# Attention scores in four 64x64 tiles of the TensorE array, router logits in four column quarters, and a guard that keeps the second tile's last weights behind the keys

## Chip, cores, metric

One core of a Trainium2 chip. The metric is device time in microseconds (us) of that core. The kernel before takes 726.5 us (median of 4 runs, 723.9 to 727.3); two runs of one kernel usually agree within 1%.

In the profile, PE is the TensorE matmul engine, PEld its weight loads, DVE, ACT and POOL the vector, scalar and GpSimd engines, SP the engine that issues most DMAs. "L375" is line 375 of that kernel's file, so one line of code has other numbers in other kernels.

## The reference, cut to what matters

```python
# attention: B=8, H=8 heads, S=576, 64 numbers a head; window 32, in half the heads with dilation 4
scores = q @ k.T / sqrt(64); scores = where(mask, scores, -1e9)
attn = exp(scores - max) / sum
x = (attn @ v) laid out as (B, S, 512)
# mixture of experts, top 1 with a locality gate: 8 experts, 512 -> 1024 -> 512
logits = x @ w_gate; local = sigmoid(x @ w_local)
e = argmax(logits) if local < 0.5 else the expert of the position before
out = softmax(logits)[e] * (relu(x @ w1[e]) @ w2[e])
```

## The kernel before

It works through 32 head pairs n, two heads on 128 partitions, in 9 blocks of 64 queries with 96 keys each. Scores go into PSUM, DVE clamps them with the mask, ACT takes the exponential, PE multiplies with the values. Every second step transposes two pairs' output for the router. Logits come per group of two batches. When the first tokens are routed, 36 dense expert tiles follow. Attention takes some 140 us, the experts some 578.

```python
def load(n):                       # issued by SP four pairs ahead
    nc.sync.dma_start(out=kq, in_=qk[n])                 # 592 KB
    nc.sync.dma_start(out=vt[WIN:]..., in_=v[n])         # 292.5 KB
    loaded[n] = kq[:, :WIN + S], kq[:, WIN + S:], vt
...
def scores(n):
    for a, z in UNITS:                                   # blocks 0..4 and 5..8
        for i in range(a, z):
            for u in range(2):                           # the two heads: rows 0..63, 64..127
                h = slice(u * DH, (u + 1) * DH)
                matmul(sc[:KW, u, block i], lhsT=kt[h, 96 keys], rhs=qt[h, 64 queries],
                       tile_position=(u * DH, 0))
        DVE: pr = min(max(sc, -CEIL), mask);  ACT: pr = exp(pr)
...
def logits(g):                     # 1152 tokens in three column tiles of 384, in two banks
    for kk in range(DK):
        for lp, b, c, s, z in parts:                     # 384 or 192 tokens
            matmul(lp[c * LW:(c + 1) * LW, ...], lhsT=wg[:, kk], rhs=xt..., tile_position=(0, c * LW))
    # four ACT copies PSUM -> le, three transposes of le by PE ("lt")
...
for n in range(NPB + 2):           # the order of PE's work
    scores(n); turn((n - 3) // 2) if n is odd; values(n - 1)
    load(n + 4)
    fetch(6 if begun[0] else 1)    # expert weights
```

## Time and profile before

| | before |
|---|---|
| median | 726.5 us |
| profiled run: span, granted clock | 726.2 us, 0.997 |
| first hidden matmul of the experts ("experts begin") | 148.6 us |
| PE busy from 9.0 us to there | 133.3 of 139.6 us |
| PE's instruction fetch | 52 packets of 16 KB |

"Experts begin": the change touches only what comes before it, and in the chain in order of time it shows as the first row of 64 matmuls for hp. The stretch starts at 9.0 us because the first pair and most of the warm-up matmuls (L335) run before.

The busy times by stretch for that whole part of the kernel before (stretch, its length; busy us and records of PE, weight load, DVE, ACT, POOL; granted clock, DMA share, GB/s), then PE's waits up to there (engine, what it was to do, what it waited for; us in all, how often, the longest), then the row of PE's instruction queue on the page:

```profile
9.00:148.60 139.60, 133.25 (x2533) 114.51 (x2533) 98.42 (x299) 72.80 (x144) 33.47 (x32) 1.00 0.86 311
```
```profile
PE sc L373 <- DVE pr L380: 1.8, 4, 0.8
PE lt L496 <- ACT le L487: 1.7, 2, 0.8
...
PE sc L373 <- issue: 0.5, 1, 0.5
```
```profile
q8 instruction: 52, 0.85, 0.5%
```

PE is idle for 6.3 us of 139.6, at full clock from 11.2 us on, where the trace's clock record begins (the first pair's scores, before that, took 3.08 us and not 1.68). One wait of 0.5 us is marked "issue": PE stood still though no semaphore held it.

### The profile page before, as it was taken

Reading aid. Unit: us, or ns where it says so; the run is one execution under the profiler, and the core shown is the slowest. Engines: PE = TensorE matmul, PEld = TensorE weight load, DVE = VectorE, ACT = ScalarE, POOL = GpSimd, SP = SyncE. Lnnn points to the kernel's source line nnn. Section 1 sums busy time; section 2 is a strip of 40 time slices with the busy share of each in tenths; the row PEclk is TensorE's granted clock in tenths of the full one; section 3 lists DMA queues with packets and bytes.
Section 4 is the critical chain, followed back from the end, with each engine's and each line's share of the span. In section 5 each row is a group of like instructions: output and inputs, shape, how many; then the busy total and the mean of one; then the engine's idle time right before and its main releaser. Section 6 shows DMA issues by size and latency. Waiting matters only on the chain.

```text
span 726.2 us, 16502 instructions
## 1 busy us (share of the span) xinstructions
PE 709.1 (98%) x6354; PEld 536.4 (74%) x6354; DVE 191.4 (26%) x554; ACT 124.2 (17%) x233; POOL 211.3 (29%) x219
## 2 busy tenths in 40 slices
PE   8999999999999999999999999999999999999995
PEld 6978787967677777667766776677667767776773
DVE  3657597742239212110010101010110101010100
ACT  2646554512000000000100000001000000000000
POOL 2222210342332324313233323332333233323100
PEclk9999999999999999999999999999999999999998
DMA  9969787951683772535594171630169116211780
GB/s 335 338 235 328 230 285 300 402 217 59 185 312 107 229 267 44 162 130 178 176 318 158 53 256 33 203 110 29 33 210 325 38 33 213 100 30 36 216 297 15
DMA packets 37590, 131.22 MB, mean 181 GB/s; under 512 B 6686, under 2 KB 6814, under 8 KB 37504
## 3 DMA queue, kind: packets, MB, share of 16 engines
q1 hardware_dynamic: 29600, 110.68, 43.2%
q0 software_dynamic: 7904, 19.41, 9.6%
q8 instruction: 52, 0.85, 0.5%
q14 instruction: 34, 0.28, 0.1%
HBM read 207.37 MB, written 19.69 MB: 313 GB/s over the span
## 4 chain that ended last, share of the span: by engine, by line
PE 90%; DVE 5%; ACT 1%; issue 1%; DMA 1%; POOL 0%; POOLq 0%; DVEq 0%; ACTq 0%
PE hp L903 34%; PE yp L931 33%; PE sc L373 6%; PE pv L426 4%; PE tp L873 2%; PE hp L897 2%; PE lp L481 2%; PE yp L927 2%; PE put L767 2%; PE tp L452 2%; DVE pr L380 1%; DMA xg<-xd,dilated 1%; PE idle L335 1%; DVE x L432 0%; DVE by_place L749 0%
## 5 line engine op out<-in xcount | busy, mean ns | idle before, releaser
L903 PEld LDWEIGHTS hp<-xe,w1s 128*128 128x128 f32 x2304 | 262.9, 192 | 16.6 <-issue 16.3
L903 PE MATMUL hp<-xe,w1s 128*128 128x128 f32 x2304 | 264.8, 275 | 0.9 <-DVE xe L875 0.9
L931 PE MATMUL yp<-w2s,h 128*128 128x512 f32 x576 | 254.3, 593 | 0.0
L931 PEld LDWEIGHTS yp<-w2s,h 128*128 128x128 f32 x576 | 106.2, 190 | 118.2 <-issue 118.1
L856 POOL DMA_INDIRECT xg<-xd,plain x76 | 73.2, 964 | 296.8 <-PE yp L931 248.3
L907 ACT ACTIVATE h<-hp 128x512 f32<-128x512 f32 x76 | 45.4, 597 | 509.3 <-PE hp L903 481.1
L856 POOL DMA_INDIRECT xg<-xd,dilated x76 | 73.0, 961 | 57.4 <-PE yp L931 51.7
L939 DVE TENSOR_SCALAR y<-yp,gate 128x512 f32<-128x512 f32 x38 | 28.5, 751 | 216.4 <-PE yp L931 102.9
L875 DVE COPY xe<-tp 128x512 f32<-128x512 f32 x38 | 26.2, 690 | 214.6 <-PE tp L873 214.6
L940 POOL DMA_INDIRECT out_dram<-y,tok x38 | 38.7, 1019 | 79.3 <-DVE y L939 75.8
L373 PE MATMUL sc<-kq 64*96 64x64 f32 x1152 | 59.2, 252 | 2.5 <-DVE pr L380 1.8
L373 PEld LDWEIGHTS sc<-kq 64*96 64x96 f32 x1152 | 53.5, 165 | 8.0 <-DVE pr L380 2.7
L380 DVE SCALAR_TENSOR_TENSOR pr<-sc,mk 96x640 f32<-96x640 f32 x64 | 47.8, 747 | 40.7 <-PE pv L426 21.4
L383 ACT ACTIVATE pr<-pr 96x640 f32<-96x640 f32 x64 | 43.8, 685 | 61.3 <-DVE pr L380 56.7
L329 POOL COPY vt<-vt 32x1040 f32<-32x1040 f32 x25 | 26.1, 1045 | 75.1 <-DMA vt<-in_v_dram 62.5
L426 PE MATMUL pv<-vt,pr 96*64 96x65 f32 x1152 | 43.6, 225 | 0.5 <-ACT xt L457 0.2
L426 PEld LDWEIGHTS pv<-vt,pr 96*64 96x64 f32 x1152 | 37.5, 137 | 7.1 <-issue 3.8
L432 DVE TENSOR_TENSOR x<-pv,rec 128x320 f32<-128x320 f32 x64 | 26.9, 453 | 0.2
L873 PE MATMUL tp<-cst,xg 128*128 128x128 f32 x152 | 23.3, 275 | 0.8 <-DMA xg<-xd,dilated 0.8
L452 PE MATMUL tp<-cst,x 128*128 128x128 f32 x144 | 19.2, 278 | 0.0
L873 PEld LDWEIGHTS tp<-cst,xg 128*128 128x128 f32 x152 | 17.6, 141 | 1.9 <-DMA xg<-xd,dilated 1.1
L463 ACT COPY xt<-tp 128x288 f32<-128x288 f32 (+2 forms) x48 | 18.4, 564 | 0.9 <-PE tp L452 0.8
(178 smaller groups left out, 240.5 us busy)
## 6 DMA issues: line engine op xcount, KB each, us to landing
w1s<-in_w_dram SPq DMA_DIRECT2D x160, 512.0 KB
w2s<-in_w_dram SPq DMA_DIRECT2D x160, 512.0 KB
kq<-in_qk_dram SPq DMA_DIRECT2D x32, 592.0 KB
vt<-in_v_dram SPq DMA_DIRECT2D x32, 292.5 KB
xd<-x SPq DMA_DIRECT2D x16, 576.0 KB
xg<-xd,plain POOLq DMA_INDIRECT x76, 2.9
xg<-xd,dilated POOLq DMA_INDIRECT x76, 2.7
out_dram<-y,tok POOLq DMA_INDIRECT x38, 4.2
```

What stands on the lines that cost most here:

```text
L373: here[:] = [nc.tensor.matmul(sc[:KW, u, (i - a) * QB:(i - a + 1) * QB], lhsT=kt[h, i * QB:i * QB + KW], rhs=qt[h, i * QB:(i + 1) * QB], s ...
L380: nc.vector.scalar_tensor_tensor(pr[:, :, :w], sc[:KW, :, :w], -CEIL, mk[:, at:at + w].unsqueeze(1).to_broadcast([KW, 2, w]), Alu.max, Alu ...
L383: nc.scalar.activation(pr[:, :, :w], pr[:, :, :w], Act.Exp, scale=SCALE)
L426: here[:] = [nc.tensor.matmul(pv[u * QB:(u + 1) * QB, i - a], lhsT=pr[:, u, (i - a) * QB:(i - a + 1) * QB], rhs=vt[:, u, i], start=True, s ...
L452: nc.tensor.transpose(tp[:, :, i], x[:, c * w + i].rearrange("p g d -> p (g d)"), ident)
L856: i = nc.gpsimd.indirect_dma_start(out=xg[t][:, kk], out_offset=None, in_=xd if full == ROWS else xd[:full], in_offset=bass.IndirectOffset ...
L873: nc.tensor.transpose(tp[:, kk], x[:, kk], ident)
L903: here[:] = [nc.tensor.matmul(hp[:, m], lhsT=w1s[ps[0] % 2][:, at, kk], rhs=x[:, kk], start=(kk == 0), stop=(kk == DK - 1))]
L907: nc.scalar.activation(ht[t][:, half * FK // 2:(half + 1) * FK // 2], hp, Act.Relu)
L931: here[:] = [nc.tensor.matmul(yp, lhsT=h[:, m], rhs=w2s[ps[0] % 2][:, m], start=(m == 0), stop=(m == FK - 1))]
L939: nc.vector.tensor_scalar(y, yp, of_tile("gate", t), None, Alu.mult)
L940: nc.gpsimd.indirect_dma_start(out=out, out_offset=bass.IndirectOffsetOnAxis(ap=of_tile("tok", t), axis=0), in_=y, in_offset=None, bounds_ ...
```

## The change

Its intent: the score matmuls use two 64x96 pieces of the array at a time. Cut into 64 keys each, they would fill four 64x64 tiles at once, with shorter weight loads. The logits use three column tiles; four equal ones would take fewer rounds. The guard is to keep the second expert tile's last weights from going ahead of the keys.

```diff
-        loaded[n] = kq[:, :WIN + S], kq[:, WIN + S:], vt
+        loaded[n] = kq, kq[:, WIN + S:], vt
 ... scores
-                    here[:] = [nc.tensor.matmul(sc[:KW, u, (i - a) * QB:(i - a + 1) * QB],
-                                                lhsT=kt[h, i * QB:i * QB + KW], rhs=qt[h, i * QB:(i + 1) * QB],
-                                                start=True, stop=True, tile_position=(u * DH, 0))]
+                    for k in (0, QB):
+                        here[:] = [nc.tensor.matmul(sc[k:k + QB, u, (i - a) * QB:(i - a + 1) * QB],
+                                                    lhsT=kt[h, i * QB + k:(i + 1) * QB + k],
+                                                    rhs=qt[h, i * QB:(i + 1) * QB], start=True, stop=True,
+                                                    tile_position=(u * DH, k), skip_group_check=True)]
 ... logits
-        lps = [bank([P, NQ], "lp") for _ in range(2)]      (three column tiles, 384 + 192 tokens)
+        m = GS // 4
+        lp = bank([P, m], "lp")
         for kk in range(DK):
+            for c in range(4):
+                b, s = divmod(c * m, S)
+                nc.tensor.matmul(lp[c * LW:(c + 1) * LW], lhsT=wg[:, kk],
+                                 rhs=st["xt"][b][:, kk // CH, s:s + m, kk % CH], start=(kk == 0),
                                  stop=(kk == DK - 1), skip_group_check=True, tile_position=(0, c * LW))
+        (six ACT copies to le in place of four)
 ... main loop
-        fetch(1 if not begun[0] else 6)
+        if begun[0] or needs[0][:2] <= (1, False):
+            fetch(6 if begun[0] else 1)
```

(The logits' removed loop is left out.)

## The prediction

> **What bounds the kernel now.** I read the page, then the chain that ended last in order of time, then the busy times by stretch, then the trace's single records around the few waits that nothing explains. First the page:
>
> ```profile
> PE 709.1 (98%) x6354; PEld 536.4 (74%) x6354; DVE 191.4 (26%) x554; ACT 124.2 (17%) x233; POOL 211.3 (29%) x219
> ...
> L373 PE MATMUL sc<-kq 64*96 64x64 f32 x1152 | 59.2, 252 | 2.5 <-DVE pr L380 1.8
> L373 PEld LDWEIGHTS sc<-kq 64*96 64x96 f32 x1152 | 53.5, 165 | 8.0 <-DVE pr L380 2.7
> ...
> L426 PE MATMUL pv<-vt,pr 96*64 96x65 f32 x1152 | 43.6, 225 | 0.5 <-ACT xt L457 0.2
> ```
>
> PE is the bound: about 141 us of attention (slices 1 to 8), then 36 expert tiles that the change leaves alone. The program has 576 score matmuls; 1152 records say that an f32 matmul runs as two passes, each with its own weight load. The chain in order of time gives the length of each piece, 36 records a head pair n:
>
> ```profile
> 23.35 0.76 PE pv L426 x20
> 24.20 0.69 DVE pr L380
> 24.89 0.16 DVE rec L431 x2
> 25.05 0.57 DVE x L432 x2
> 25.62 0.14 issue
> 25.77 0.82 DVE pr L380
> 26.61 0.74 ACT pr L383
> 27.35 0.76 ACT xt L463 x2
> 28.15 0.69 PE pv L426 x16
> 28.84 1.68 PE sc L373 x36
> ...
> 36.22 1.17 PE sc L373 x24
> 37.38 0.50 issue
> 37.88 0.72 PE sc L373 x12
> 38.60 1.20 PE pv L426 x36
> ```
>
> Scores take 1.68 us a pair, values 1.20, transposes 1.13 in every second step. Two steps are 2 x 1.68 + 2 x 1.20 + 1.13 = 6.89 us of PE, and the chain's real pace is some 7.15. To see: in the step with a transpose (24.20 to 28.15) the chain leaves PE for DVE and ACT, and at 37.38 PE stands still with no semaphore awaited, in the middle of 36 like matmuls. That second wait is what I rest the prediction on.
>
> ```profile
> 29.00:42.00 13.00, 12.47 (x266) 11.44 (x265) 8.98 (x23) 6.37 (x12) 4.18 (x4) 1.00 1.00 381
> 42.00:58.00 16.00, 14.98 (x263) 11.48 (x263) 8.67 (x32) 9.14 (x20) 2.09 (x2) 1.00 0.63 214
> 98.00:114.00 16.00, 14.02 (x296) 12.59 (x296) 15.84 (x60) 8.31 (x17) 1.04 (x1) 1.00 0.89 315
> ```
>
> (Stretches: busy us of PE, weight load, DVE, ACT, POOL; clock; DMA share; GB/s.) DMA is nearly full while keys and values stream in, and DVE is full from 98 to 114.
>
> **What the Trainium skill says.** "TensorE: Matmul & The Clock Gate", section LDWEIGHTS: a weight load takes its columns divided by 1.2 GHz. The trace agrees: score records start in couples 6 ns apart (the two row tiles), and couples follow each 85 ns, with 96 columns (96/1.2 = 80, plus 5); the half tiles of L897 with 64 columns follow each 58 ns. "TensorEngine Tiling (Array Packing)", section Tiling Modes: 64x64 gives four tiles that load and compute on their own. Before shows only two or three at once: in the logits, parts in three column tiles start at 115.737, 115.743 and 115.750. "Runtime: NRT & Kernel Launch", section Instruction fetch mechanics: instructions come in 16 KiB blocks of 256, two blocks held, the next fetched while one runs, and this is mostly hidden. The trace agrees on the blocks and not on the hiding (below). "DMA: Bandwidth & Descriptors", section Queues, rings and completion order: an engine takes turns between its queues by packet. The trace shows fetch packets far later than one turn.
>
> **The instruction fetch.** The wait at 37.88 begins exactly 256 PE records after a like one at 31.10. PE's instruction queue moved one 16 KB packet from 28.67 to 29.81 and one from 35.53 to 36.54: PE went on 1.29 and 1.34 us after each. A third such wait stands in L897's dense half tiles, where DMA is quiet (packet end 706.91, on at 708.25, again 1.34):
>
> ```profile
> 37.88 0.56 PE L373 MATMUL sc<-kq 64*96 64x64 f32 x8 [0.50 <-issue]
> ```
> ```profile
> 708.25 0.92 PE L897 MATMUL hp<-xe,w1s 128*64 128x64 f32 x24 [0.45 <-issue]
> ```
>
> Laying the packets beside each 256th record of the trace, every block has its own packet, which starts after the block before has begun, and no block starts earlier than 1.29 us after its packet's end. From a block's begin to the next packet's start passes 1.05 us in the quiet case (708.25 to 709.30), 4.43 and 4.89 in the two attention stalls, 2.9 in the mean of the 20 attention blocks. It waits behind data: the packet at 42.77 came as the keys issued at 37.49 were landing (42.9). So a block can't take less than lag + 1.0 (packet) + 1.3: 3.35 us quiet, some 5.2 at the mean lag, 7 at worst. Now an attention block lasts 6.9 us, so this is hidden but for two waits.
>
> **The change part by part.** *Scores.* 1152 records of 96 weight columns become 2304 of 64, in four tiles. If four passes start together, a round takes 58 ns in place of 85; 18 rounds a pair: 18 x 27 = 0.48 us off, 1.68 becomes 1.20. Over 31 pairs 14.9 us of PE work; the first, at half clock (3.08 us), gives some 0.9 more. Not all of it can reach the end: in transpose steps the DVE-ACT chain above (3.95 us, nothing in it shortened) already sets the pace, so I allow 0.2 of 0.48 there. 15 x 0.48 + 16 x 0.2 = 10 us. *Logits.* Four tiles of 288 columns in place of 384 + 192 per tile: 8 rounds of some 250 ns for 8 of 340, 0.7 us a group; but the last rounds wait for ACT's copies of xt, and six copies out in place of four add 0.35 us of ACT (four took 1.5). Four groups at some 0.4: 1.6 us. *Weights behind the keys.* The compiled order of DMA issues on SP is the same, line for line, before and after: the new condition is never false where it would matter. Worth 0. Without anything else the sum is 10 + 0.9 + 1.6 = 12.5: 714 us.
>
> *What it adds.* 2304 more PE records (1152 matmuls, 1152 loads). Two steps hold 310 PE instructions now (144 scores, 144 values, 18 transposes, some 4 semaphore waits) and 454 after: 1.77 blocks for 1.21. From 13.9 to the experts' begin at 148.6 now run 19.6 blocks in 134.7 us; after, 28.3. Own work left: (134.7 - 10) / 28.3 = 4.4 us a block. Fetch: if PE slows, DMA has more air; I estimate the lag at 2.5, so 4.9 us a block. The longer of the two, both scattering by about 1 us, is some 5.1 in the mean: 28.3 x 5.1 = 145 us, 10 more than now. Less 1.6 and some of the 0.9: 726.2 + 10 - 2 = 734, and I say 735. The PE time gained is real but instructions arrive too slowly for it.
>
> **Rivals.** (a) *Fetch stays hidden*: lag falls to the quiet 1.05 us as the pace changes, a block needs only 3.35, and the gain is DVE-limited: 713 to 717. For it: the quiet lags are short, and waits for logits let DMA drain. Against: the streaming bytes are the same, and already now two blocks stalled. (b) *Four tiles run only in couples*: a round takes 2 x 58 = 116 ns, scores 2.2 us a pair, 31 x 0.56 = 17 us more: 743. Against it: three column tiles started within 13 ns in the logits. (c) *Fetch is worse than I think*: lag stays at 3.5, a block 5.8: 28.3 x 5.8 = 164, 29 more: 753. (d) *DMA bound*: two steps move 2 x (592 + 292.5) + 576 KB = 2.4 MB, 6.3 us at the 381 GB/s of the full stretch. That is below today's 7.15, and keys land 6 to 13 us before use from n = 4 on, so it takes a part of the gain at most: 716 to 718.
>
> **Range and chances.** The middle is 735; (a) and (d) draw the range to 716, (c) and (b) to 750. Faster by over 2% means under 711.7, beyond even (a) in full: 0.07. Slower by over 2% means over 740.7, a lag of 2.8 rather than 2.5: 0.29. Within: 0.64.
>
> **What would show it.** Right: in the score groups 2304 records, rounds of four starts some 6 ns apart and 58 ns a round; PE waits marked "issue" in attention rising from 2 to over ten, each 256 PE records apart and ending 1.3 us after a fetch packet; some 9 more fetch packets before the experts; the experts' first hidden matmuls later than 148.6; tile times there unchanged at 7.14 and 6.87 us. Wrong: those waits stay few and the experts start at 136 to 140 (rival a), or score pairs take over 2 us without "issue" waits (rival b), or PE waits for kq or vt (rival d).

## The result, and the profile after

Changed: 750.3 us (median of 4 runs, 747.8 to 752.2), against 726.5 before in the same rounds. The ratio of the fast runs is 1.033, 95% interval 1.029 to 1.038: slower. (A ratio here is the mean time of one kernel's fast runs over that of the other's of the same rounds, so not quite the ratio of the medians quoted.) Executions over 1.5% slower than the fastest of the same kernel are left out of the means. The result lies 0.3 us above the predicted range.

The page of the changed kernel:

```profile
span 746.0 us, 18811 instructions
...
PE 702.5 (94%) x7506; PEld 528.5 (71%) x7506; DVE 192.4 (26%) x554; ACT 125.8 (17%) x241; POOL 210.9 (28%) x219
...
q8 instruction: 61, 1.00, 0.5%
...
L375 PE MATMUL sc<-kq 64*64 64x64 f32 x2304 | 49.7, 235 | 18.2 <-issue 16.2
L375 PEld LDWEIGHTS sc<-kq 64*64 64x64 f32 x2304 | 42.7, 146 | 25.0 <-issue 17.5
L429 PE MATMUL pv<-vt,pr 96*64 96x65 f32 x1152 | 48.2, 240 | 6.9 <-issue 4.7
```

PE is busy for 6.6 us less than before, and the program is 20 us longer. The score groups have twice the records, and 18.2 us of idle time before them where there were 2.5. The instruction queue moved 9 packets more. The same three views as before:

```profile
9.00:169.50 160.50, 127.54 (x3646) 108.98 (x3645) 99.02 (x298) 73.46 (x149) 33.12 (x32) 0.91 0.76 273
```
```profile
PE sc L375 <- issue: 16.2, 10, 3.5
PE pv L429 <- issue: 4.7, 3, 2.8
PE lt L497 <- ACT le L488: 2.6, 2, 1.3
PE lp L481 <- ACT xt L466: 2.2, 3, 0.9
```

PE idles for 33.0 us of 160.5; 13 waits marked issue make up 20.9 of them. The second thing to see is the clock, 0.91 where it was 1.00. The chain in order of time shows both (start, length, what; x72 is one pair's scores, x36 its values):

```profile
9.22 1.21 PE sc L375 x72
...
16.90 0.96 PE sc L375 x53
17.86 3.54 issue
21.40 0.90 PE sc L375 x19
22.30 2.11 PE tp L455 x9
24.41 2.15 PE pv L429 x36
...
33.73 1.21 PE sc L375 x72
34.94 0.73 PE pv L429 x18
35.66 2.83 issue
38.49 0.29 PE pv L429 x3
...
169.54 7.38 PE hp L904 x64
```

A pair's scores take 1.21 us where nothing disturbs them: the four tiles do run at once (in the single records, four starts some 7 ns apart, then the next four 58 ns after the first). But at 17.86 PE stops in the middle of a pair for 3.54 us, and the transposes and values after it take 2.11 and 2.15 us where they need 1.13 and 1.20. The stretches around that place say why:

```profile
16.80:20.21 3.41, 1.06 (x57) 0.89 (x53) 2.12 (x6) 1.51 (x3) 1.77 (x2) 1.00 1.02 400
20.21:27.04 6.83, 5.64 (x84) 5.07 (x88) 1.21 (x4) 2.01 (x4) 1.37 (x2) 0.50 0.23 90
27.04:30.45 3.41, 3.41 (x173) 3.21 (x166) 2.88 (x9) 1.50 (x3) 0.17 (x1) 1.00 0.74 229
```

In the first stretch DMA is full (share 1.02) and PE starves; in the next 6.83 us the granted clock is 0.50; then it is full again. The expert phase is as long as before: 746.0 - 169.5 = 576.5 us, against 726.2 - 148.6 = 577.6. So the whole loss is made before the experts begin.

### The profile page after: what moved, and what is told of

It reads as the page before. It is cut to its first block, busy times and chain, and to the rows that moved or that the text cites.

```text
span 746.0 us, 18811 instructions
## 1 busy us (share of the span) xinstructions
PE 702.5 (94%) x7506; PEld 528.5 (71%) x7506; DVE 192.4 (26%) x554; ACT 125.8 (17%) x241; POOL 210.9 (28%) x219
## 4 chain that ended last, share of the span: by engine, by line
PE 87%; DVE 6%; issue 4%; ACT 3%; POOL 0%; POOLq 0%; DVEq 0%; ACTq 0%
PE hp L904 33%; PE yp L932 32%; PE pv L429 5%; PE sc L375 5%; PE tp L874 2%; PE hp L898 2%; PE yp L928 2%; PE put L768 2%; DVE pr L383 2%; ACT xt L466 1%; PE tp L455 1%; ACT pr L386 1%; DVE x L435 1%; PE idle L335 1%; PE lp L481 1%
## 5 line engine op out<-in xcount | busy, mean ns | idle before, releaser
L375 PE MATMUL sc<-kq 64*64 64x64 f32 x2304 | 49.7, 235 | 18.2 <-issue 16.2
L375 PEld LDWEIGHTS sc<-kq 64*64 64x64 f32 x2304 | 42.7, 146 | 25.0 <-issue 17.5
L429 PE MATMUL pv<-vt,pr 96*64 96x65 f32 x1152 | 48.2, 240 | 6.9 <-issue 4.7
L429 PEld LDWEIGHTS pv<-vt,pr 96*64 96x64 f32 x1152 | 41.9, 151 | 13.6 <-issue 7.5
L455 PE MATMUL tp<-cst,x 128*128 128x128 f32 x144 | 21.4, 298 | 0.2 <-DVE x L435 0.2
L455 PEld LDWEIGHTS tp<-cst,x 128*128 128x128 f32 x144 | 17.2, 151 | 1.5 <-DVE x L435 0.4
```

What stands on the lines that cost most here:

```text
L375: here[:] = [nc.tensor.matmul(sc[k:k + QB, u, (i - a) * QB:(i - a + 1) * QB], lhsT=kt[h, i * QB + k:(i + 1) * QB + k], rhs=qt[h, i * QB:(i ...
L429: here[:] = [nc.tensor.matmul(pv[u * QB:(u + 1) * QB, i - a], lhsT=pr[:, u, (i - a) * QB:(i - a + 1) * QB], rhs=vt[:, u, i], start=True, s ...
L455: nc.tensor.transpose(tp[:, :, i], x[:, c * w + i].rearrange("p g d -> p (g d)"), ident)
```

## The experiments

Three theories were to be told apart. *Fetch*: the added PE records make blocks of 256 instructions follow faster than the fetch delivers them behind keys and values. *Tiles*: the four tiles, or the logits' new form, hold PE up themselves. *Clock*: whatever makes PE idle also halves its clock, and that takes what was saved. The table sums up the runs' profiles from 9.0 us to the experts' begin. "Half clock" is the time in that stretch for which the trace's clock record says 0.50.

| kernel | experts begin | PE busy | PE idle | of it "issue" | half clock |
|---|---|---|---|---|---|
| before | 148.6 | 133.3 | 6.3 | 0.5 | 0 |
| changed | 169.5 | 127.5 | 33.0 | 20.9 | 27.3 |
| scores_only | 176.0 | 135.8 | 31.2 | 20.1 | 41.0 |
| logits_only | 151.8 | 133.9 | 8.9 | 0.5 | 10.2 |
| half | 155.7 | 130.4 | 16.3 | 6.8 | 10.2 |
| before_noload | 147.6 | 130.4 | 8.1 | 0 | 0 |
| after_noload | 148.7 | 120.6 | 19.1 | 3.8 | 10.2 |
| scores_noload | 152.3 | 120.9 | 22.4 | 9.2 | 0 |
| after_halfload | 167.8 | 130.0 | 28.8 | 12.8 | 34.1 |
| after_onepass | 148.7 | 116.3 | 23.4 | 4.1 | 64.9 |
| before_onepass | 142.6 | 117.3 | 16.2 | 0 | 51.3 |
| before_onepass_fill | 159.7 | 146.5 | 4.2 | 0 | 0 |

Each row is one profiled run. In the kernels whose result is wrong the routing differs, so only the part before the experts counts.

Two things blur small differences between rows. The runs came in four rounds on four chips, and the kernel before had medians of 726.8, 731.5, 727.5 and 730.2 us in them. And the start is not alike: the second pair's scores begin at 11.9 us in the profiled run of the kernel before and at 8.5 to 10.1 us in the other rows. Counted from there to the experts' begin, the kernel before takes 136.8 us, the changed kernel 160.3, before_noload 138.6, after_noload 138.9, scores_noload 142.7 and logits_only 141.7. Differences of under some 5 us between rows are no more than hints.

### Which part of the change costs: scores_only, logits_only

Each takes one part of the diff above into the kernel before: the scores (with the `loaded[n]` line) or the logits. The guard got no run: the 404 DMA issues of SP come in the same order in the traces of both kernels.

> Only the scores in four tiles, logits and weights as before. Fetch theory (the scores' 2304 more PE records make instruction blocks of 256 follow faster than they can be fetched behind the keys and values): 747 to 754 us, as slow as the whole change or 1 to 2 us slower; some 13 PE waits marked issue with about 20 us in attention, experts' first hidden matmul at 169 to 172 us. Rival (the logits' new form, or ACT's two more copies a group, hold up the chain): this kernel is at 714 to 728 us, with the experts at 137 to 150 us.

> Only the logits in four column quarters. It has no more PE records than before (256 fewer at most). Prediction's sum: 1.6 us faster, so 724 to 726.5 us. Fetch theory: no new issue waits (1 to 3), so nothing lost. Rival (the logits are what costs): 735 us or more.

scores_only: 753.2 us, ratio 1.036 (1.031 to 1.041), 12 issue waits. It is as slow as the whole change; its experts begin at 176.0 us, later than the 169 to 172 expected.

```profile
PE sc L374 <- issue: 16.5, 10, 2.9
PE pv L428 <- issue: 3.6, 2, 2.5
```

logits_only: 731.0 us, ratio 1.003 (1.000 to 1.006), so the same, and none of the 1.6 us expected. The runs scatter with their clock: the four fast ones have 725.6 us at 0.997 and 730.5 to 731.2 at 0.984 to 0.990; the other two, 736.5 and 739.6 us at 0.981 and 0.976, count as slow and are left out of the ratio. The rounds of four column quarters follow each other every 250 ns, as predicted, but the last of them still wait for ACT's copies, and the transposes after them wait 2.6 us in two groups, where they waited 1.7. In the profiled run (731.2 us) PE then idled through more than a third of a window, and this followed (stretches as above):

```profile
44.90:48.40 3.50, 2.19 (x53) 1.87 (x51) 2.02 (x8) 2.39 (x7) 0.20 (x1) 1.00 0.00 0
48.40:58.70 10.30, 10.30 (x129) 9.61 (x127) 4.78 (x19) 3.87 (x7) 2.09 (x2) 0.50 0.66 236
58.70:65.00 6.30, 6.30 (x138) 5.82 (x136) 5.63 (x17) 2.34 (x4) 1.04 (x1) 1.00 0.70 220
```

Ten microseconds at half clock, and the waits in the window before are for ACT, not for fetch. So the clock can fall without a fetch wait.

### Fetch with nothing in its way: before_noload, after_noload

```diff
+    kqs = [once.tile([P, WIN + 2 * S], F32, name=f"kq{i}") for i in range(ahead + 1)]
-        kq = ins.tile(...);  nc.sync.dma_start(out=kq, in_=qk[n])
+        kq = kqs[n % len(kqs)]
+        if n < len(kqs):
+            nc.sync.dma_start(out=kq, in_=qk[n])          # values likewise
```

> The kernel before with the keys and values loaded for the first five head pairs only, and the buffers used again for the later ones (wrong result on purpose; the routing and so the experts differ, the comparison is of attention up to the experts' first hidden matmul, 148.6 us before). Fetch theory: its two issue waits (1 us) go, experts at 144 to 149 us. A DMA-bound theory: experts well below 144.

> The changed kernel with the keys and values loaded for the first five head pairs only (wrong result on purpose), instruction count unchanged. Fetch theory: without the data in the way a block's packet starts 1.0 to 1.6 us after the block before, a block needs 3.4 to 4.2 us, issue waits in attention drop from 13 with 20.9 us to under 4 with under 3 us, the halved clock goes with them, and the experts begin at 128 to 142 us where the changed kernel has 169.5: the change is then a gain of 5 us or more over the same form of the kernel before. Rival (four tiles, or PE's own issue of twice as many instructions, cost the time by themselves): issue waits stay, experts at 160 us or later.

Measured 147.6 and 148.7 us. For the changed kernel that is 20.9 us earlier, with the same instructions and tiles; the kernel before gains 1.0 from the same edit, and nothing if its late start is taken off (138.6 us against 136.8 from the second pair on). PE's waits of the changed kernel without loads:

```profile
PE sc L379 <- DVE pr L387: 4.3, 7, 1.0
PE sc L379 <- issue: 3.8, 4, 1.9
PE lt L501 <- ACT le L492: 2.6, 2, 1.3
PE lp L485 <- ACT xt L470: 2.6, 3, 1.0
```

Issue waits fall from 13 with 20.9 us to 4 with 3.8. From the single records: the mean time from a block's begin to the start of the next block's packet is 2.4 us with all loads and 1.3 without (2.9 and 0.6 in the kernel before). So the fetch packets do wait behind the data, and taking the data out of their way takes the loss away. Of the 20.9 us, 17.1 are issue waits and 7.0 PE busy time (127.5 against 120.6; the clock, below), and 3.2 come back as more other waits.

The expectation missed in its other half: the begin at 148.7 is not in 128 to 142, the issue waits are not quite under 4 with under 3 us, and 10.2 us at half clock stayed. PE is busy for 9.8 us less than in before_noload and idle for 11.0 more. Even with most of the fetch waits gone, the change shows no gain, in one run of each.

### Fewer of them: half

```diff
+                    if exact or n % 2:
+                        (the one 96-key matmul of before)
+                        continue
                     for k in (0, QB):
```

> Four tiles only in the even steps, which have no transposes; logits as before. Half of the added PE records (1152), so some 24 blocks in attention and not 28. Fetch theory: steps with four tiles lag and the others catch up, issue waits 3 to 8 with 4 to 12 us in all, experts' first hidden matmul at 149 to 160 us, 727 to 740 us: less than half of the loss of the whole (26 us of scores alone). Rival (the loss goes with each four-tile score, whatever the blocks do): half of it, 739 to 742 us. If the fetch stayed hidden in those steps: a gain, 718 to 724 us.

739.6 us, ratio 1.015 (1.010 to 1.021), experts at 155.7; 8 issue waits, 6.8 us:

```profile
PE sc L379 <- issue: 3.2, 5, 1.2
...
PE sc L374 <- issue: 1.9, 1, 1.9
PE pv L433 <- issue: 1.7, 2, 1.4
```

L374 here is the old form, in the odd steps: it waits too, since it follows a step that ran ahead. With none, half and all of the added records, issue waits are 0.5, 6.8 and 20.1 us (all: scores_only): half the dose gives a third. On total time the two theories had touching ranges (727 to 740, and 739 to 742), so this run does not separate them; a ratio of 1.015 is a little under half of 1.036.

### Half of the data: after_halfload

As after_noload, but every second pair is loaded.

> The changed kernel with the keys and values of every second head pair after the fifth loaded (wrong result on purpose), a dose between all (14 waits for fetch, 20.4 us of them before the experts, which begin at 169.5 us) and none (3 and 1.9 us, at 148.7). Fetch theory (packets queue behind data): waits for fetch 5 to 10 with 4 to 12 us, experts at 151 to 162 us. Rival (a threshold: any loading at all brings the waits): as with all, 165 us or later.

Issue waits: 8, with 12.8 us, between 3.8 and 20.9, and a lag of 1.8 us between 1.3 and 2.4. The number of waits is as the fetch theory says, their time a little over its 12 us. But the experts begin at 167.8, outside the 151 to 162 and inside the rival's 165 or later:

```profile
PE sc L379 <- issue: 9.3, 6, 2.4
PE sc L379 <- DVE pr L387: 5.5, 6, 2.9
PE pv L433 <- issue: 3.5, 2, 2.8
```

Of the 19.1 us more than in after_noload, 9.0 are issue waits and 9.4 PE busy time for the same work, with 34.1 us at half clock against 10.2. The waits and the lag lie between all and none, which speaks against a threshold, but the begin does not: fetch waits alone do not size the loss.

### The number of records or the tiles: after_onepass, before_onepass, before_onepass_tiny

Scores from the upper halves of the numbers, read as bf16, take one pass where f32 takes two, so half the records. The result is coarser on purpose. (It still passes with this case's inputs; that says nothing about other inputs.)

```diff
+        kb, qb = (t.bitcast(BF16).rearrange("p (s two) -> p s two", two=2) for t in (kt, qt))
-                      lhsT=kt[h, keys],    rhs=qt[h, queries]
+                      lhsT=kb[h, keys, 1], rhs=qb[h, queries, 1]
```

> The changed kernel with scores in the same four 64x64 tiles, but of the upper halves of the numbers as bf16 in one pass (result wrong or coarse on purpose): the score records fall to the number of the kernel before (1152 matmuls and 1152 loads), while all keys and values are loaded. Fetch theory: count, not tiles, is what costs, so waits for fetch are 0 to 4 with under 5 us and the experts begin at 140 to 152 us. Rival (tiles conflict with loads, or four tiles slow the chain by themselves): experts at 160 us or later.

> The kernel before with scores from the upper halves as bf16 in one pass, two tiles as before (coarser on purpose): 1152 fewer PE records than before, some 0.9 us less PE work a pair. Fetch theory: no waits for fetch but one or two. Theory of the clock: idle PE brings half-clock windows (19 in the four-tile one-pass kernel), which take most of the saving: 720 to 731 us, clock 0.95 to 0.98. Rival (attention's chain through DVE and ACT is the floor and the clock costs nothing): the same time, so only the next run tells these apart.

after_onepass has four tiles, all loads, and the record count of the kernel before. The experts begin at 148.7, and issue waits are 4.1 us: the tiles by themselves do not bring the waits. (This kernel also has less PE work, so it is no clean swap of the count alone.)

```profile
9.00:148.66 139.66, 116.28 (x2505) 96.90 (x2494) 98.71 (x298) 72.92 (x148) 33.01 (x32) 0.77 0.85 314
```

But PE, with 17 us less to do than in the kernel before, is no earlier, and its clock is 0.77. before_onepass, with 1152 records fewer again, has no issue wait and begins the experts at 142.6. It takes 719.2 us, ratio 0.987 (0.983 to 0.992), just under the 720 to 731 expected and the only kernel here faster than the one before, at clock 0.96 to 0.97. It beats both, at the price of coarser scores, and not by the 2% that would be called faster.

```diff
+                    for _ in range(3):      # before_onepass_tiny: 54 more matmuls a pair
+                        nc.tensor.matmul(sc[KW:KW + 1, u, 511:512], lhsT=bb[h, :1], rhs=bb[h, :1],
+                                         tile_position=(u * DH, KW), ...)
```

> The one-pass kernel in two tiles with 54 matmuls of one number by one number a pair beside its 18, so that the score records are as many as in the changed kernel (72 and 72 a pair), with no 64-column tiles. PE work per tiny matmul is not known; at some 30 ns it is 1.6 us a pair, so PE work is about that of the kernel before. Fetch theory (the number counts): issue waits in attention 8 to 16 with 10 to 25 us, experts at 155 to 180 us; before_onepass had none and 142.6. Rival (the four tiles cost, not the number): under 4 issue waits, experts at 140 to 150 us. If the tiny matmuls take 60 ns or more, PE is the bound and nothing is told.

The tiny matmuls slowed PE to 334.6 us of attention, at half clock for 242 of them; the last case of the expectation holds and nothing is told.

### The price of the halved clock: before_onepass_fill, after_noload_fill

```diff
+            fill(bk[:, 5 * VW:], 2)        # ahead of each half of the values: two matmuls of zeros
```

> The same with four matmuls of zeros a pair (0.86 us of PE) ahead of the values, into unused columns of their banks, where PE waits for ACT. Theory of the clock: under six half-clock windows, experts earlier than in before_onepass by 3 us or more though PE has more to do, 710 to 724 us. Rival (the chain through DVE and ACT is the floor): no earlier, or later by up to 10 us.

> The changed kernel without loads after the fifth pair (wrong result on purpose), with the fillers of both: 0.86 us of zeros a pair and 1.7 us a group of logits. Without loads and fillers it had 5 waits for fetch (4.5 us), three half-clock windows (at most 5 us lost), 13 us of other waits and began the experts at 148.7 us. Theory of the clock: no or one half-clock window, experts at 141 to 149 us. Rival (the fillers' own time is the larger): 150 us or later.

The zeros were mis-sized: some 1.8 us a pair and not 0.86 (54.7 us in the stretch). So 740.0 us and experts at 159.7, later than both theories allowed, and the kernel as such loses. The profile is worth reading all the same, here with before_onepass first:

```profile
9.00:142.56 133.56, 117.33 (x1960) 98.93 (x1954) 97.46 (x298) 71.17 (x142) 33.19 (x32) 0.81 0.89 328
```
```profile
9.00:159.69 150.69, 146.54 (x2219) 117.75 (x2220) 102.47 (x298) 71.65 (x142) 33.05 (x32) 1.00 0.81 288
```

With PE kept busy the clock never falls in this stretch. What a halved clock costs PE can be read from the same work in both: scores, values and transposes take 19.9 + 46.2 + 19.5 = 85.6 us here and 25.0 + 50.1 + 25.8 = 100.9 in before_onepass. So 51.3 us at half clock cost some 15 us of PE time, an estimate of 0.30 us for each. Two other pairs give 0.35 (the changed kernel against scores_noload) and 0.46 (logits_only against the kernel before). How much of that reached the end in before_onepass, where PE also waits for others, this run cannot say. after_noload_fill had PE full of zeros (experts at 184.0 us) and tells nothing more.

### Zeros around the logits: logits_fill, logits_fill2

Nine matmuls of zeros a group, in the logits' two waits.

> Only the logits in four column quarters, and nine matmuls of zeros into unused columns of their banks at the two places where PE waits for ACT there (about 1.7 us a group, in waits of 1 and 1.3 us). Theory of the clock (a 3.41 us window with over some 1.3 us of idle PE halves the clock for the next one; that is what made the logits-only kernel scatter from 725.6 to 739.6 us): no half-clock windows after the logits, clock at 0.994 or more in every run, all runs within 724 to 728 us. Rival (the scatter has another cause, or six ACT copies cost by themselves): runs over 730 us remain.

> The logits in four column quarters with the same nine matmuls of zeros a group, the first four now into a bank of their own, so the result is right. The broken run began its experts at 148.8 us with no half-clock window, logits_only at 151.75 with three. Theory of the clock: clock 0.994 or more in every run, 724 to 728.5 us in every run. Rival (the ACT copies cost by themselves): 729 us and more, or scatter as in logits_only (725.6 to 739.6).

logits_fill gave a wrong result, and so another routing and 796 us. Its zeros went into unused columns of the bank in which the logits were being summed; logits_fill2, with those zeros in a bank of their own, is correct. In both profiled runs there was no half-clock window before the experts (148.8 and 149.0 us). But logits_fill2 takes 739.2 us, ratio 1.011 (1.007 to 1.016), its fast runs from 734.0 (clock 0.997) to 743.9 (0.987), with one of 748.0 counted as slow, and the expected 0.994 in every run did not come. In its profiled run the expert phase is 7.6 us longer than in the kernel before (734.2 - 149.0 against 726.2 - 148.6 us), most of it before 206 us, where the fourth group's zeros run too. So zeros are no cure here, and why its other runs lost clock stays open.

### Four tiles without loads or logits: scores_noload

scores_only with the edit of after_noload.

> Four-tile scores with the logits of before, keys and values loaded for the first five pairs only (wrong result on purpose). Fetch theory: at most 4 issue waits with under 4 us, experts far below the 176 us of the loaded one (scores_only). The prediction's rival a (fetch hidden, 10 us of gain): experts at 136 to 142 us. If the saved PE time is taken by other waits and the clock: 143 to 149 us, where before_noload has 147.6.

Experts at 152.3 us, outside all three ranges: 23.7 earlier than with loads, and 4.7 later than before_noload (4.1 from the second pair on, one run each, on two chips). The stretch is all at full clock:

```profile
9.00:152.26 143.26, 120.89 (x3647) 101.25 (x3646) 99.61 (x298) 71.63 (x143) 32.77 (x32) 1.00 0.39 149
```

(The record of the kernel before without loads, for comparison: 130.44 us busy of 138.57.) The four tiles save 9.5 us of PE time (the scores alone 11.2: 44.6 us for 55.8), and 14.3 us more idle time comes in: 9.2 of it still marked issue (8 waits, twice the 4 waits and 4 us expected), the rest mostly waits for DVE and ACT. The saving is real in PE's own time and reaches the end in no run of the f32 form.

### When the clock falls

Thirteen traces have 3.41 us windows at full clock before the experts. By PE's idle time in such a window, this is how often the next window was at half clock:

| idle in the window | windows | next one at half clock |
|---|---|---|
| under 0.5 us | 333 | 1 |
| 0.5 to 1.3 | 113 | 7 |
| 1.3 to 1.5 | 16 | 10 |
| over 1.5 | 23 | 20 |

All half-clock stretches last one or more whole windows of 3.41 us. The kernel before has none: no window of it has over 0.9 us of idle PE. A fetch wait of 2 to 3.5 us lies above. This is a count; the test is before_onepass_fill, where filling PE's idle time took all half-clock windows away.

## Why the prediction was wrong, and where it was right

- **Direction and mechanism: right.** The added instructions are fetched too slowly behind the data. The signs named came: 13 issue waits ("over ten"), 9 more packets, experts later, a pair's scores at 1.21 us (1.20 expected), expert tiles as before. The eleven longest of the waits lie whole multiples of 256 PE instructions apart (weight loads, matmuls and semaphore waits counted together) and end 1.3 to 1.6 us after a packet. Of 28 block starts up to 164.4 us, 16 come within 1.5 us of their packet's end, none earlier than 1.27. Taking the loads away removed the loss (after_noload); the old record count with the same tiles had none either (after_onepass).
- **The number of blocks and the lag: right.** 28.3 blocks were predicted and 28 intervals are there from 9.4 to 164.4 us. The lag was estimated at 2.5 us and is 2.4.
- **The failing step** is the mean of the longer of own work and fetch: "some 5.1 in the mean: 28.3 x 5.1 = 145 us". Measured: 5.54 us a block. 28 x 0.44 = 12.3 us, most of the 15 between 735 and 750. The fetch side held: the 16 blocks that the fetch ended last 5.28 us in the mean (2.9 of the 12.3 us). The own work was mis-sized: the other 12 blocks, for which I had allowed 4.4 us, last 5.88, from 3.1 to 8.4, and make 9.4 of the 12.3. (The term was small even by its own numbers: spreads of 1 us about 4.4 and 4.9, taken as normal and independent, give 5.2 for the longer, an estimate.)
- **What the own work left out: that it is uneven, and the halved clock.** The three longest blocks (from 47.0, 91.4 and 130.5 us; 8.32, 8.39 and 7.90 us) hold the router's logits, with 1.05 us of half clock among them; they are 9.3 us over three times 5.1, and the short blocks after two of them give 3.7 back. Three more (21.4 to 27.7, 80.3 to 86.9, 154.0 to 160.5 us) lie for the most part in half-clock stretches that follow a window in which PE had stood for 0.8 to 2.4 us; they are 4.0 us over. With the loads gone, block lengths still spread by 1.4 us (standard deviation, after_noload and scores_noload), where the prediction took 1. How the loss divides between the two, no run shows.
- **PE's time was saved, but less of it, and the clock took much back.** At full clock the scores' PE time fell by 11.2 us (scores_noload), not 14.9. In the changed kernel scores, values and transposes take 115.9 us, in scores_noload 106.3: the 27.3 us at half clock cost some 10 us of PE time, and the waits took more than the rest.
- **The gain of 10 us on the other side of the scale did not show.** The prediction had 714 us without the fetch, and 713 to 717 in rival (a). With the loads gone, after_noload and scores_noload begin the experts 1.1 and 4.7 us later than before_noload. PE's saved time turned into waits for DVE, ACT and what is left of the fetch.
- **Two readings in the prediction go too far.** "Far later than one turn" holds only if a turn is one packet of the trace; the last section says why that is open. And not every packet starts after the block before has begun: in the kernel before one of 19 starts 0.1 us earlier, in the changed kernel two of 28, next to logits, 0.2 and 1.1 us earlier.
- **Rivals.** (b), four tiles only in couples: fell, 1.21 us a pair. (d), DMA bound: fell, no wait of PE in the changed kernel's attention is for keys or values, and before_noload gains at most 1.0 us. (c), 5.8 us a block and 753 us, was nearest in size, for another reason than the one it gave: the lag stayed at 2.4.
- **Logits, 1.6 us: wrong.** The rounds shrank to 250 ns as worked out, but ACT's copies end the block and two more copies lengthen the wait after it: 0, or a loss by the clock. **Guard, 0:** as predicted from the compiled order; no run tested it.

What stays open: how much of the changed kernel's loss the clock makes by itself. It cannot be held at full speed there, since zeros are instructions too and would come through the same fetch. And what makes up the 2.4 us that a packet waits behind data.

## What to carry to other kernels

Count the instructions of a dense stretch as well as its busy time: 256 records in less than the time that a fetch takes behind full data queues (here some 5 us) is a bound of its own, and splitting work into smaller tiles doubles the count. Look for waits marked "issue" in the kernel before; one of 0.5 us was the warning. And where PE is the bound, a saving that leaves it idle for over some 1.3 us in 3.4 can halve its clock, so look at the granted clock by stretch and not at the mean.

## What the Trainium skill lacked or had wrong

- "Runtime: NRT & Kernel Launch", section Instruction fetch mechanics: the fetch is "mostly hidden", and PE's instruction memory is given both as 128 KiB and as two 16 KiB lines. In the changed kernel all but two of 28 packets start only after the block before has begun, no block starts earlier than 1.27 us after its packet's end, and PE waits 20.9 us of 160.5 for fetch.
- "DMA: Bandwidth & Descriptors", section Queues, rings and completion order: not shown to be wrong, but it lacks what the turns cost an instruction fetch. The lag to a fetch packet's start was 2.4 us in the mean with loads and 1.3 without, up to 4.1 in the changed kernel. The page gives 9 to 17 descriptors as typical for the packet of a turn; if a data record of the trace (4.7 KB, 0.18 us) is one descriptor, that is 1.6 to 3.1 us, an estimate that the lag fits. No run shows where such packets end.
- "TensorE: Matmul & The Clock Gate", section What's actually happening: free windows of 3413 ns and two states, and the traces agree (half-clock stretches of 3.41, 6.83, 10.24 us). That the slow state comes after a whole idle window of about 3.4 us does not fit: 20 of 23 windows with over 1.5 us of idle PE, and 10 of 16 with 1.3 to 1.5, were followed by half clock.
